# Decode attention over a 512 MiB cache: from a ring of six 32 KiB slots to a ring of three 64 KiB slots

## The chip, the cores and the metric

One core of a Trainium2 chip; the other cores are idle. Its engines go by short names here: PE (TensorE, matrix products), DVE (VectorE), ACT (ScalarE), Pool (GpSimd) and SP (SyncE, which issues the transfers). A descriptor is one contiguous piece of a transfer; the trace shows each as a packet, with its size and its time on one of the 16 DMA engines. A transfer has landed when the last of these engines has counted up its semaphore, the counter that the other engines wait for.

The metric is the device time of one execution in microseconds (us), median of several. Executions of one kernel in one session agree within 0.2%. "Span" is the profile's time from the first to the last instruction, some 2 us less than the device time.

## The reference, cut to what matters

One token, 32 heads, 32768 cached positions of 128 values in bf16. K and V are 256 MiB each; all weights together are about 17 MB.

```python
def reference(A_x, A_k_cache, A_v_cache, A_wq, A_wo, B_x, B_w_gate, B_w_up, B_w_down):
    ...
    xn = _layernorm(x, axis=-1)
    # per head: scores = q . k * Dh**-0.5; p = softmax(scores); o = p . v; then o @ wo
    return x + _A_ref(xn, A_k_cache, A_v_cache, A_wq, A_wo) + _B_ref(xn, B_w_gate, B_w_up, B_w_down)
```

## The kernel before

The cache streams through a ring of slots in SBUF. Partition p holds positions 256 p to 256 p + 255 of a head, 64 KiB of contiguous memory for K and as much for V. SP issues the transfers in order, each as soon as its slot's last user is done:

```python
    CH = 128                      # positions of a partition in one slot: 32 KiB
    NCH = NJ // CH                # 2 slots per head of K, 2 of V
    SLOTS = 6
    SCR = 2                       # score buffers
    TAIL = [64, 32, 16, 16]       # the last V slot comes in four pieces
    ...
                for u in units:   # wq, ffn, then k and v alternating, wo, the last v
                    s = slot_of[u]
                    for o in ([s] if u[0] in ("k", "v") else [s, s + 1]):
                        if o in owner:
                            e.wait_ge(*owner.pop(o))
                    ...
                    elif u[0] == "k":
                        _, h, c = u
                        e.dma_start(ring[:, s, :], kv_src(A_k_cache, h, c * CH, CH)).then_inc(s_slot[s], 16)
                        owner[s] = (s_qk, NHF * (h * NCH + c + 1))
```

The DVE multiplies K by q in place, 64 positions at a time. The PE sums groups of the 128 products by matmuls with an identity matrix, the DVE reduces the rest. After the last chunk of a head the DVE takes the maximum, the PE transposes and spreads it, and ACT does the exp. The PE's order:

```python
                for k in range(NK):
                    scores(k)
                    h, c = divmod(k, NCH)
                    if c < NCH - 1:
                        if h >= 1:
                            total(h - 1)          # denominator of the previous head
                            pv(h - 1, c)          # its V chunk
                        continue
                    if h >= 1:
                        halves = pv_ops(h - 1, c)
                        next(halves)              # first half of the V chunk
                    turn(h)                       # transpose of the maximum
                    if h >= 1:
                        next(halves)              # second half
                    spread(h)
                    if h >= 2:
                        fold(h - 2)
                fold(H - 2)
                t.wait_ge(s_wo, 16)
                t.wait_ge(s_ov, H - 1)
                for h in range(H - 1):
                    att(h)                        # output projection, 5 matmuls per head
                total(H - 1)
                for c in range(NCH):
                    pv(H - 1, c)                  # last V: 256 matmuls of one column
                t.wait_ge(s_ov, H)
                att(H - 1).then_inc(s_att, 1)
```

## Time and profile before

| | before |
|---|---|
| median time | 1302.45 us (1302.35 to 1302.62) |
| span of the profiled run | 1300.05 us |
| PE busy, DVE busy | 81%, 52% |
| rate of transfers, 100 to 1100 us | 431 to 432 GB/s |
| last data landed, from the start | 1295.44 us |
| from there to the end | 4.61 us |

The page of the kernel before: the span; the busy share of the 16 DMA engines in 40 slices, in tenths; what they moved; the packets; the queue's share of the engines' time.

```profile
span 1300.1 us, 9523 instructions
...
DMA  9999999999999999999999999999999999999997
GB/s 396 428 426 435 433 429 428 433 435 427 435 429 434 427 433 431 432 429 433 432 432 425 434 433 431 431 430 436 428 430 432 433 430 429 433 432 430 429 407 315
DMA packets 23960, 554.60 MB, mean 427 GB/s; under 512 B 2480, under 2 KB 6640, under 8 KB 6896
...
q1 hardware_dynamic: 23920, 554.00, 99.5%
```

The engines that carry the transfers are busy in every slice until the last, and 99.5% of their time goes to the one queue. While every engine is busy, the stream can end sooner only if its packets take less time in all. The chain that ended last, by engine and by line:

```profile
DMA 51%; PE 32%; DVE 16%; SPq 1%; issue 0%; DVEq 0%; ACT 0%
DMA ring<-in_A_k_cache_dram 47%; PE ps L233 18%; DVE ring L488 15%; PE ps L279 10%; DMA ring<-in_B_w_down_dram 2%; DMA ring<-in_A_v_cache_dram 2%; PE ps L250 2%; PE ps L330 1%; PE ps L321 0%; SPq L190 0%; PE ps L315 0%; PE ps L338 0%; SPq L185 0%; SPq L195 0%; DVE sc L496 0%
```

The DVE and PE steps in this chain are how a slot comes free for the next transfer. They do not slow the stream here, because the queue holds several transfers: in the packet records at least 15 packets are in flight at any time between 60 and 1240 us. Two groups of instructions (busy us, mean ns of one | idle before, and what ended it):

```profile
L488 DVE TENSOR_TENSOR ring<-ring,qb 128x8192 bf16<-128x8192 bf16 x128 | 560.6, 4421 | 117.0 <-DMA ring<-in_A_k_cache_dram 117.0
...
L279 PE MATMUL ps<-ring,P 128*4 128x512 bf16 x1984 | 443.3, 379 | 0.0
```

The DVE waits 117 us in all for K. That is the sign of compute with time to spare.

The end of the timeline (start, duration, engine, line; in brackets the idle time before and what ended it). It shows the last V's 256 matmuls and the issue of the output:

```profile
1285.74 3.55 PE L275 MATMUL ps<-P,ring 128*128 128x1 bf16 x128 [3.02 <-DMA ring<-in_A_v_cache_dram]
...
1290.57 1.01 PE L275 MATMUL ps<-P,ring 128*128 128x1 bf16 x32 [1.28 <-DMA ring<-in_A_v_cache_dram]
...
1292.20 1.86 PE L275 MATMUL ps<-P,ring 128*128 128x1 bf16 x64 [0.61 <-issue]
...
1295.49 0.58 PE L275 MATMUL ps<-P,ring 128*128 128x1 bf16 x16 [0.65 <-DMA ring<-in_A_v_cache_dram]
...
1296.98 0.35 SPq L202 DMA_DIRECT2D out_dram<-outb  x1
```

The PE follows the last pieces as they land, and the output leaves 1.54 us after the last of them (1296.98 - 1295.44).

The trace also records every packet's size and duration. In the kernel before:

```text
bytes    4096   8192   16384   17280   32768   40960
ns        159    309     611     644    1216    1514     (median)
```

### The profile page before, as it was taken

The numbers are of one execution on the slowest core, as the hardware profiler recorded it, in microseconds if no ns is written. First come the engines' busy times: TensorE is split into PE (matmuls) and PEld (weight loads), VectorE is DVE, ScalarE is ACT, GpSimd is POOL, SyncE is SP. The second block draws the span as 40 slices with busy tenths as digits, with TensorE's granted clock in tenths as the row PEclk, the third lists the DMA queues.
The fourth block names the chain that finished last, engine by engine and source line by source line (L and its number), as shares of the span: only waits on it lengthen the run. The fifth ranks groups of instructions, "written<-read, shape, count | busy, mean of one in ns | idle before, by whom it ended". The sixth has DMA issues, their size and how long they took to land.

```text
span 1300.1 us, 9523 instructions
## 1 busy us (share of the span) xinstructions
PE 1056.5 (81%) x5142; PEld 261.4 (20%) x3222; DVE 678.1 (52%) x406; ACT 50.8 (4%) x139; POOL 1.1 (0%) x8
## 2 busy tenths in 40 slices
PE   3678888888887887887887887887887888878886
PEld 1311122211212211211211211211211211212215
DVE  0465566456455466456455455455456455456450
ACT  2000000000000000000000000000000000000000
POOL 0000000000000000000000000000000000000000
PEclk9689899988989989889988899988899998989996
DMA  9999999999999999999999999999999999999997
GB/s 396 428 426 435 433 429 428 433 435 427 435 429 434 427 433 431 432 429 433 432 432 425 434 433 431 431 430 436 428 430 432 433 430 429 433 432 430 429 407 315
DMA packets 23960, 554.60 MB, mean 427 GB/s; under 512 B 2480, under 2 KB 6640, under 8 KB 6896
## 3 DMA queue, kind: packets, MB, share of 16 engines
q1 hardware_dynamic: 23920, 554.00, 99.5%
q8 instruction: 33, 0.54, 0.2%
q14 instruction: 7, 0.06, 0.0%
HBM read 553.99 MB, written 0.00 MB: 426 GB/s over the span
## 4 chain that ended last, share of the span: by engine, by line
DMA 51%; PE 32%; DVE 16%; SPq 1%; issue 0%; DVEq 0%; ACT 0%
DMA ring<-in_A_k_cache_dram 47%; PE ps L233 18%; DVE ring L488 15%; PE ps L279 10%; DMA ring<-in_B_w_down_dram 2%; DMA ring<-in_A_v_cache_dram 2%; PE ps L250 2%; PE ps L330 1%; PE ps L321 0%; SPq L190 0%; PE ps L315 0%; PE ps L338 0%; SPq L185 0%; SPq L195 0%; DVE sc L496 0%
## 5 line engine op out<-in xcount | busy, mean ns | idle before, releaser
L488 DVE TENSOR_TENSOR ring<-ring,qb 128x8192 bf16<-128x8192 bf16 x128 | 560.6, 4421 | 117.0 <-DMA ring<-in_A_k_cache_dram 117.0
L233 PE MATMUL ps<-ring,ident 128*128 128x512 bf16 x1920 | 508.6, 425 | 0.0
L279 PE MATMUL ps<-ring,P 128*4 128x512 bf16 x1984 | 443.3, 379 | 0.0
L279 PEld LDWEIGHTS ps<-ring,P 128*4 128x4 bf16 x1984 | 163.4, 85 | 346.7 <-issue 109.4
L250 PE MATMUL ps<-ring,ident 128*128 128x512 bf16 x128 | 55.7, 435 | 209.0 <-DVE ring L488 209.0
L496 DVE TENSOR_REDUCE sc<-ps 128x64 f32<-128x512 f32 x128 | 88.3, 690 | 243.8 <-PE ps L233 243.8
L250 PEld LDWEIGHTS ps<-ring,ident 128*128 128x128 bf16 x128 | 12.6, 98 | 518.8 <-DVE ring L488 421.5
L412 ACT ACTIVATE P<-sc,negb 128x256 bf16<-128x256 f32 x32 | 16.3, 508 | 1186.1 <-DVE negb L511 1186.1
L511 DVE TENSOR_SCALAR negb<-ps 128x1 f32<-128x1 f32 x32 | 5.0, 158 | 108.4 <-PE ps L321 108.4
L506 DVE TENSOR_REDUCE m<-ps 1x1 f32<-1x128 f32 x32 | 8.9, 279 | 81.6 <-PE ps L315 81.6
L309 PEld LDWEIGHTS ps<-rsum,ones 128*128 128x128 f32 x64 | 12.3, 194 | 104.8 <-issue 104.0
L300 PE MATMUL ps<-identf,o 4*128 4x1 f32 x248 | 31.8, 245 | 0.9 <-ACT o L395 0.9
L300 PEld LDWEIGHTS ps<-identf,o 4*128 4x128 f32 x248 | 30.0, 187 | 0.9 <-ACT o L395 0.9
L225 PE MATMUL ps<-ring 128*128 128x512 bf16 x40 | 11.5, 461 | 11.9 <-DMA ring<-in_A_wq_dram 11.9
L395 ACT ACTIVATE o<-ps,rzb 4x512 f32<-4x512 f32 x31 | 21.0, 677 | 0.0
L457 DVE TENSOR_SCALAR sg<-sg 128x13 f32<-128x13 f32 (+1 forms) x2 | 0.2, 158 | 35.0 <-ACT sg L388 35.0
L503 DVE TENSOR_REDUCE pmax<-sc 128x1 f32<-128x256 f32 x32 | 13.4, 420 | 1.1
L315 PE MATMUL ps<-identf,pmax 128*1 128x128 f32 x64 | 12.2, 272 | 1.2 <-DVE pmax L503 1.2
L321 PE MATMUL ps<-m,ones 1*128 1x1 f32 x64 | 12.1, 256 | 0.4 <-DVE m L506 0.4
L330 PE MATMUL ps<-xn,ring 128*128 128x1 bf16 (+1 forms) x140 | 8.8, 198 | 4.4 <-DMA ring<-in_B_w_down_dram 4.4
L275 PE MATMUL ps<-P,ring 128*128 128x1 bf16 x256 | 7.6, 165 | 5.7 <-DMA ring<-in_A_v_cache_dram 5.1
L321 PEld LDWEIGHTS ps<-m,ones 1*128 1x128 f32 x64 | 9.4, 182 | 14.2 <-issue 13.5
(47 smaller groups left out, 85.7 us busy)
## 6 DMA issues: line engine op xcount, KB each, us to landing
ring<-in_A_k_cache_dram SPq DMA_DIRECT2D x64, 4096.0 KB, 44.5
ring<-in_A_v_cache_dram SPq DMA_DIRECT2D x63, 4096.0 KB, 47.1
ring<-in_A_wq_dram SPq DMA_DIRECT2D x1, 5120.0 KB, 15.5
ring<-in_A_wo_dram SPq DMA_DIRECT2D x1, 5120.0 KB, 43.0
ring<-in_B_w_gate_dram SPq DMA_DIRECT2D x1, 2160.0 KB, 20.2
ring<-in_B_w_up_dram SPq DMA_DIRECT2D x1, 2160.0 KB, 24.8
ring<-in_B_w_down_dram SPq DMA_DIRECT2D x1, 2080.0 KB, 28.6
ring<-in_A_v_cache_dram SPq DMA_DIRECT2D x1, 2048.0 KB, 21.3
```

Source lines behind the costliest of these rows:

```text
L233: return t.add_instruction(mybir.InstMatmult(start_tensor_calc=False, stop_tensor_calc=stop, tile_size=(128, 128), tile_position=(0, 0), l ...
L250: t.matmul(ob, lhsT=ident[:, :], rhs=src, start=True, stop=False)
L279: mm = t.matmul(O[h % 2], lhsT=P[:, h % PR, jj:jj + W], rhs=ring[:, s, j * DH:(j + W) * DH], start=(jj == 0), stop=(jj + W == NJ))
L300: mm = t.matmul(fold_ps, lhsT=o4[:, m * DH:(m + 1) * DH], rhs=identf[0:W, m:m + 1], start=(m == 0), stop=(m == W - 1))
L309: t.matmul(misc[:, 129:130], lhsT=ones[:, :], rhs=rsum[:, h % SR:h % SR + 1], start=True, stop=True).then_inc(s_z, 1)
L321: t.matmul(misc[:, 128:129], lhsT=ones[0:1, :], rhs=m1[0:1, h % SR:h % SR + 1], start=True, stop=True).then_inc(s_b, 1)
L330: mm = t.matmul(misc[0:n, off + j:off + j + 1], lhsT=hidden(w, c, j), rhs=xn[:, c:c + 1], start=(c == 0), stop=(c == NCD - 1))
L395: a.activation(out=o4[:, :], in_=O[h % 2], func=ACTF.Copy, scale=rzb[0:W, h % SR:h % SR + 1]).then_inc(s_o4, 1)
L412: a.activation(out=P[:, h % PR, :], in_=sc[:, h % SCR, :], func=ACTF.Exp, bias=negb[:, h % SR:h % SR + 1], scale=c_scale, accum_out=rsum[: ...
L488: v.tensor_tensor(out=kh, in0=kh, in1=q[:, None, :].to_broadcast([128, HF, DH]), op=ALU.mult).then_inc(s_mul, 1)
L496: v.tensor_reduce(out=sc[:, h % SCR, j:j + HF], in_=bank[n % NBK].rearrange("p (j e) -> p j e", e=G), axis=AX.X, op=ALU.add).then_inc(s_re ...
L503: v.tensor_reduce(out=pmax[:, h % SR:h % SR + 1], in_=sc[:, h % SCR, :], axis=AX.X, op=ALU.max).then_inc(s_max, 1)
```

## The change

Intent: fewer, larger transfers. One slot now holds a whole head of K or of V, so each partition's 64 KiB is one descriptor and there are half as many. The ring's size stays (3 x 64 KiB), the order of the stream stays. Weights take one slot instead of two. The second score buffer goes, and total(h - 1) moves ahead of the V products.

```diff
-    CH = 128
+    CH = NJ
...
-    SLOTS = 6
+    SLOTS = 3
...
-    SCR = 2
+    SCR = 1
...
-    TAIL = [64, 32, 16, 16]
+    TAIL = [128, 64, 32, 16, 16]
...
-    pos = 0
-    for u in units:
-        wide = 1 if u[0] in ("k", "v") else 2
-        assert wide == 1 or pos % 2 == 0
+    for pos, u in enumerate(units):
         s = pos % SLOTS
         slot_of[u] = s
-        pos += wide
...
                     if h >= 1:
+                        if NCH == 1:
+                            total(h - 1)
                         halves = pv_ops(h - 1, c)
                         next(halves)
                     turn(h)
```

More of the change, by code (lines that the diff above doesn't have):

```diff
@@ L134, in bass_parallel_sum__gqa_block_cached__swiglu_ffn__decode_kernel @@
         xnb = flat[:, x0:x0 + NCD * 128].rearrange("p (c m) -> p c m", c=NCD)
-        assert NCD * (H * DH + 128) <= 2 * CE
+        assert NCD * (H * DH + 128) <= CE
         wq_v = wq.rearrange("p (c n) -> p c n", c=NCD)
@@ L141, in bass_parallel_sum__gqa_block_cached__swiglu_ffn__decode_kernel @@
         wd = flat[:, d0:d0 + FB * D].rearrange("p (j d) -> p j d", j=FB)
-        assert 2 * NCD * F + FB * D <= 2 * CE
+        assert 2 * NCD * F + FB * D <= CE
         wg_v = wg.rearrange("p (c n) -> p c n", c=NCD)
@@ L152, in bass_parallel_sum__gqa_block_cached__swiglu_ffn__decode_kernel @@
         wo_v = wo.rearrange("p h (m c) -> p h m c", c=NCD)
-        assert H * D <= 2 * CE and NCD * H * DH <= 2 * CE
+        assert H * D <= CE
         def kv_src(cache, h, j0, n):
@@ L171, in sp @@
                     s = slot_of[u]
-                    for o in ([s] if u[0] in ("k", "v") else [s, s + 1]):
-                        if o in owner:
-                            e.wait_ge(*owner.pop(o))
+                    if s in owner:
+                        e.wait_ge(*owner.pop(s))
                     if u[0] == "wq":
                         e.dma_start(wq, A_wq.rearrange("(p c) n -> p (c n)", c=NCD)).then_inc(s_wq, 16)
-                        owner[s] = owner[s + 1] = (s_q, NQB)
+                        owner[s] = (s_q, NQB)
                     elif u[0] == "k":
@@ L197, in sp @@
                         e.dma_start(wd[0:FL, FM, :], B_w_down[FM * 128:F, :]).then_inc(s_ffn, 16)
-                        owner[s] = owner[s + 1] = (s_fpd, 1)
+                        owner[s] = (s_fpd, 1)
                     else:
```

## The prediction

> **What bounds the kernel now.** The transfers. The profile's DMA row reads nine tenths in 39 of 40 slices, queue 1 holds 99.5% of the 16 engines' span, and the rate is 430 to 433 GB/s in every 100 us from 100 to 1200 us (stage table). The chain of waits is 47% K transfers. Compute has room: PE 81%, DVE 52%. In the timeline two heads take 77.7 us (DVE product at 1174.3 and 1252.0), 38.86 us per head of 16.8 MB. Where the data is already there (113.4 to 148.4 us) a head takes 35.0 us.
>
> **What it removes.** In the trace's packet records a descriptor's time is a straight line: 4096 B 159 ns, 8192 B 309, 16384 B 611, 17280 B 644, 32768 B 1216 (fastest 1211), 40960 B 1514. The slope is 27.2 bytes/ns per engine, the intercept 8 to 9 ns. The Trainium skill, "DMA: Bandwidth & Descriptors", section "Where 436 GB/s comes from", gives 435.2 GB/s for 16 ports, the same 27.2 each; this trace agrees. So the bytes are at the ceiling and only the fixed 8.5 ns per descriptor, plus 9 ns per semaphore write, can be saved. 16,256 descriptors of 32 KiB become about 8,130: per engine 500 x 8.5 ns = 4.3 us, and 60 semaphore writes x 9 ns = 0.6 us. Expected gain 5 us, 0.4%, all on the critical path. A 64 KiB descriptor should take about 2418 ns (estimate from the line) against 2 x 1216.
>
> **What it moves.** Estimated loop of one head after, from the product's start: four products 17.5 us, the PE step after the last 3.6, denominator 0.4, first half of PV 7.1, transpose 0.3, second half 7.1, spread and bias 0.6: 36.6 us, against 38.7 between K landings. Slower than 35.0, because the DVE no longer multiplies under the first PV, but 2 us under the transfers. V lands 19.4 us after K, the PE wants it at 21.6: no new wait on average. A K slot comes free 21 us after it landed and is wanted after 39; a V slot after 17, wanted after 39. The queue never runs empty; some 15 us of backlog are tolerated. The single score buffer waits for an exp that ended before the next K landed: free.
>
> **Ends.** The first K lands at about 52 us instead of 42, but the engines stay busy meanwhile. At the end the PE leaves the last whole PV later (36.6 us after K31 landed); the output projection (6.4 us) ends at 47 us, the first V31 piece lands at 44, the last at 54. 256 products at 28 ns are 7.1 us: the tail may grow by 0.3 to 1 us.
>
> **Prediction.** 1302.45 - 4.9 + 0.5 = 1298 us; 8 times in 10 within 1295 to 1302. Chances: faster by over 2% 0.01, within 2% 0.96, slower 0.03.
>
> **What would show it.** K packets of 65,536 B at about 2418 ns; DMA rate about 433 GB/s in the middle; heads 38.7 us apart; DVE waits for K of 1 to 3 us once per head; first product at about 52 us; tail after the last landing within 1 us of now.
>
> **What would make it wrong.** A 64 KiB row cut into smaller descriptors (no gain, about 1302). PE steps slowed: its granted clock falls to 0.66 after idle gaps, and 2 us more per head would make compute the bound (each us past 38.7 costs 30 us). V landing late under the PE's in-order wait, which would hold back the transpose, the bias and the next head's products.

## The result, and the profile after

Median 1299.47 us (1299.21 to 1299.63, 4 runs), before 1302.5 us in the same session (the three runs above and a fourth of 1302.55). The ratio is 0.9977, 95% interval 0.9959 to 0.9994. Ratios here are the mean time of one kernel's runs over that of the other's of the same rounds, so not quite the ratio of the medians.

| | before | after |
|---|---|---|
| median time | 1302.5 us | 1299.47 us |
| span | 1300.05 | 1297.31 |
| last data landed | 1295.44 | 1290.41 |
| from there to the issue of the output | 1.54 | 3.33 |
| from that issue to the end | 3.07 | 3.57 |
| first K product | 46.25 | 52.42 |
| from head to head, mean of heads 10 to 30 | 39.01 | 38.86 |

The same lines of the page, after:

```profile
span 1297.3 us, 9428 instructions
...
DMA  9999999999999999999999999999999999999997
GB/s 399 435 434 425 441 431 435 428 435 431 441 425 433 433 436 431 427 439 427 447 421 435 435 427 445 421 443 426 435 435 427 443 423 439 429 438 429 433 395 288
DMA packets 14887, 554.59 MB, mean 427 GB/s; under 512 B 1472, under 2 KB 5632, under 8 KB 5888
...
q1 hardware_dynamic: 14848, 554.00, 99.2%
```

There are 9073 packets fewer, and the rate in the middle is 432 to 434 GB/s instead of 431 to 432 (table of stages, 200 us each). The slices swing more (421 to 447); a packet is now 2.4 us long, and with packets of 0.6 us (split4, below) the slices stay within 426 to 429. In the packet records 8064 packets of 65,536 bytes have a median of 2421 ns. The chain, and the two groups:

```profile
DMA 52%; PE 30%; DVE 15%; issue 3%; SPq 0%; ACT 0%; DVEq 0%
DMA ring<-in_A_k_cache_dram 52%; PE ps L274 17%; DVE ring L485 14%; PE ps L228 10%; PE ps L245 1%; PE ps L270 1%; PE ps L340 1%; PE ps L310 0%; PE ps L304 0%; PE ps L295 0%; SPq L190 0%; DVE sc L493 0%; PE ps L316 0%; ACT o L392 0%; SPq L192 0%
```

```profile
L485 DVE TENSOR_TENSOR ring<-ring,qb 128x8192 bf16<-128x8192 bf16 x128 | 557.8, 4419 | 91.6 <-DMA ring<-in_A_k_cache_dram 91.6
...
L274 PE MATMUL ps<-ring,P 128*4 128x512 bf16 x1984 | 438.3, 379 | 0.0
```

The DVE's wait for K is now 91.6 us over 30 heads, 3 us each. One head in the middle of the run shows the new order of work:

```profile
732.65 17.43 DVE L485 TENSOR_TENSOR ring<-ring,qb 128x8192 bf16<-128x8192 bf16 x4 [4.26 <-DMA ring<-in_A_k_cache_dram]
...
750.36 3.40 PE L228 MATMUL ps<-ring,ident 128*128 128x512 bf16 x15
...
753.79 0.33 SPq L185 DMA_DIRECT2D ring<-in_A_v_cache_dram  x1
...
753.81 7.07 PE L274 MATMUL ps<-ring,P 128*4 128x512 bf16 x32
...
760.93 7.07 PE L274 MATMUL ps<-ring,P 128*4 128x512 bf16 x32
...
768.35 0.16 DVE L508 TENSOR_SCALAR negb<-ps 128x1 f32<-128x1 f32 x1 [6.93 <-PE ps L316]
...
771.45 17.43 DVE L485 TENSOR_TENSOR ring<-ring,qb 128x8192 bf16<-128x8192 bf16 x4 [2.94 <-DMA ring<-in_A_k_cache_dram]
```

The four products take 17.4 us, the PE step after the last ends at 753.8, and the K slot is given to the next V at 753.79. Then come two halves of V products, and the bias at 768.35. The loop has 2.94 us to spare before the next K lands. The end of the run:

```profile
1282.88 4.62 PE L270 MATMUL ps<-P,ring 128*128 128x1 bf16 x160
...
1290.12 2.72 PE L270 MATMUL ps<-P,ring 128*128 128x1 bf16 x96 [2.62 <-issue]
...
1293.74 0.35 SPq L197 DMA_DIRECT2D out_dram<-outb  x1
```

The data was there: the pieces landed at 1280.56, 1285.50, 1287.92, 1289.16 and 1290.41. Matmul 160 lies in the middle of the second piece, and yet the PE stood still before it for 2.62 us. The transfers gained 5.03 us, and the tail gave back 2.29.

### The profile page after: what moved, and what is told of

Read it like the earlier page. It is cut to its first block, busy times and chain, and to the rows that moved or that the text cites. A ratio compares the mean times of both kernels' runs of the same rounds, so it can differ in the third digit from the quotient of the medians.

```text
span 1297.3 us, 9428 instructions
## 1 busy us (share of the span) xinstructions
PE 1036.7 (80%) x5142; PEld 263.8 (20%) x3222; DVE 669.7 (52%) x406; ACT 50.8 (4%) x139; POOL 1.1 (0%) x8
## 4 chain that ended last, share of the span: by engine, by line
DMA 52%; PE 30%; DVE 15%; issue 3%; SPq 0%; ACT 0%; DVEq 0%
DMA ring<-in_A_k_cache_dram 52%; PE ps L274 17%; DVE ring L485 14%; PE ps L228 10%; PE ps L245 1%; PE ps L270 1%; PE ps L340 1%; PE ps L310 0%; PE ps L304 0%; PE ps L295 0%; SPq L190 0%; DVE sc L493 0%; PE ps L316 0%; ACT o L392 0%; SPq L192 0%
## 5 line engine op out<-in xcount | busy, mean ns | idle before, releaser
L485 DVE TENSOR_TENSOR ring<-ring,qb 128x8192 bf16<-128x8192 bf16 x128 | 557.8, 4419 | 91.6 <-DMA ring<-in_A_k_cache_dram 91.6
L228 PE MATMUL ps<-ring,ident 128*128 128x512 bf16 x1920 | 495.3, 416 | 0.0
L274 PE MATMUL ps<-ring,P 128*4 128x512 bf16 x1984 | 438.3, 379 | 0.0
L245 PE MATMUL ps<-ring,ident 128*128 128x512 bf16 x128 | 56.2, 439 | 228.8 <-DVE ring L485 228.6
L274 PEld LDWEIGHTS ps<-ring,P 128*4 128x4 bf16 x1984 | 166.1, 85 | 245.3
L493 DVE TENSOR_REDUCE sc<-ps 128x64 f32<-128x512 f32 x128 | 82.2, 683 | 62.1 <-PE ps L228 62.1
L473 DVE RECIPROCAL rzb<-ps 128x1 f32<-128x1 f32 x32 | 5.0, 157 | 9.8 <-PE ps L304 9.8
```

The source lines that it names most:

```text
L228: return t.add_instruction(mybir.InstMatmult(start_tensor_calc=False, stop_tensor_calc=stop, tile_size=(128, 128), tile_position=(0, 0), l ...
L245: t.matmul(ob, lhsT=ident[:, :], rhs=src, start=True, stop=False)
L274: mm = t.matmul(O[h % 2], lhsT=P[:, h % PR, jj:jj + W], rhs=ring[:, s, j * DH:(j + W) * DH], start=(jj == 0), stop=(jj + W == NJ))
L485: v.tensor_tensor(out=kh, in0=kh, in1=q[:, None, :].to_broadcast([128, HF, DH]), op=ALU.mult).then_inc(s_mul, 1)
L493: v.tensor_reduce(out=sc[:, h % SCR, j:j + HF], in_=bank[n % NBK].rearrange("p (j e) -> p j e", e=G), axis=AX.X, op=ALU.add).then_inc(s_re ...
```

## The experiments

Eleven kernels, all correct, all built from the changed one.

### 1. Is it the descriptors? Cutting the loads again

The slots stay; only the load of a slot is cut. split2, split4 and split16 use PARTS = 2, 4, 16 transfers of 32, 16 and 4 KiB per partition:

```diff
-    e.dma_start(ring[:, s, :], kv_src(A_k_cache, h, c * CH, CH)).then_inc(s_slot[s], 16)
+    for i in range(PARTS):
+        n = CH // PARTS
+        e.dma_start(ring[:, s, i * n * DH:(i + 1) * n * DH],
+                    kv_src(A_k_cache, h, c * CH + i * n, n)).then_inc(s_slot[s], 16)
...
-    v.wait_ge(s_slot[s], 16 * use_of[u])
+    v.wait_ge(s_slot[s], 16 * PARTS * use_of[u])
```

(The same for V and the PE's wait.) stride2 has the descriptors of split4 in the number of transfers of split2, because each transfer takes every other piece:

```diff
+    for b in range(2):
+        e.dma_start(ring[:, s, :].rearrange("p (a b n) -> p b a n", a=2, b=2)[:, b],
+                    kv_src(A_k_cache, h, c * CH, CH).rearrange("p (a b n) -> p b a n", a=2, b=2)[:, b]
+                    ).then_inc(s_slot[s], 16)
```

Expected of split2:

> The changed kernel with its three 64 KiB slots, but each 8 MiB load issued as two transfers of 32 KiB per partition. Theory A (the gain is the fixed time of each descriptor): per engine and load 16 x 1213 + 2 x 9 ns = 19.43 us against 19.35 now, over 63 loads +4.6 us: last V landing back at about 1295 us from the start, time about 1304 us, which is slower than the kernel before, because the longer tail (6.9 us after the last landing, 4.6 before) stays. Theory B (the gain comes from the slots or from fewer waits of the queue): heads stay 38.70 us apart, time about 1299.5.

Of split4:

> The same with four transfers of 16 KiB per partition. Theory A: per engine and load 32 x 611 + 4 x 9 ns = 19.59 us, +0.235 us over 63 loads = +14.8 us: time about 1314. Theory B: about 1299.5. Theory C (the fixed cost is that of a transfer and its semaphore, not of a descriptor): from two to four transfers adds as much again as from one to two did.

Of stride2:

> Two transfers per 8 MiB load, each of which carries every other 16 KiB piece of a partition: as many transfers as split2, as many and as large descriptors as split4. Theory A: about 1.1 us less than split4, time about 1313. Theory C (cost per transfer): as split2, about 1304.

Of split16:

> Sixteen transfers of 4 KiB per partition for each load. Theory A: 128 x 159 + 16 x 9 ns = 20.50 us per load, +1.15 us over 63 loads = +72 us: time about 1371, heads about 41.0 us apart. Any theory without a cost per descriptor: below 1310. If the sequencer cannot issue sixteen transfers in 20 us (16 x 0.33 to 0.44 us = 5 to 7 us, estimate), the transfers would show gaps and the time would be above 1390.

Measured (before: 1302.21 us, timed beside these four):

| kernel | descriptor | transfers per load | packet, median | last landing | time | ratio to before |
|---|---|---|---|---|---|---|
| changed | 64 KiB | 1 | 2421 ns | 1290.41 us | 1299.47 us | 0.9977 |
| split2 | 32 KiB | 2 | 1216 ns | 1295.50 us | 1303.44 us | 1.0011 |
| split4 | 16 KiB | 4 | 614 ns | 1305.15 us | 1313.01 us | 1.0083 |
| stride2 | 16 KiB | 2 | 615 ns | 1305.02 us | 1312.82 us | 1.0082 |
| split16 | 4 KiB | 16 | 162 ns | 1361.02 us | 1367.57 us | 1.0502 |

The rate by slices of split4, then of split16 with its packets:

```profile
GB/s 388 427 428 427 429 426 428 427 429 427 428 427 427 427 428 428 428 427 428 427 429 427 428 428 426 428 427 429 427 428 428 428 427 427 429 428 426 429 403 300
```

```profile
GB/s 386 409 410 409 409 409 409 410 409 410 409 410 408 409 409 410 409 409 409 410 409 409 410 409 409 409 410 409 410 409 409 410 409 409 410 409 409 409 399 319
DMA packets 150975, 554.72 MB, mean 406 GB/s; under 512 B 16592, under 2 KB 20752, under 8 KB 150032
```

Theory A holds over a range of sixteen. Each of the 63 loads has 8 descriptors per engine in the changed kernel, so split2 adds 8 x 63 = 504 to each engine and split16 adds 120 x 63 = 7560. The last landing moves by 5.09 and 70.61 us, which is 10.1 and 9.3 ns per descriptor; split4 gives 14.74 / 1512 = 9.7 ns. Theory B falls: with three slots and 32 KiB descriptors the last V lands at 1295.50, where the kernel before had it (1295.44). So the ring of three slots neither gained nor cost anything in the stream. Theory C falls: stride2 lies with split4 (0.2 us apart), not with split2. The share I gave to semaphore writes, 9 ns each, should have put stride2 1.1 us under split4; 0.13 us at the last landing is all that shows. Within that, the fixed time belongs to the descriptor.

### 2. Is the compute loop really off the critical path?

Idle matmuls on a free PSUM bank, between the transpose and the second half of V, n = 7 or 18 per head:

```diff
+    for i in range(n):
+        if i == 0:
+            t.matmul(bank[0], lhsT=ident[:, :], rhs=qb[:, 0:512], start=True, stop=False)
+        else:
+            again(bank[0], ident[:, :], qb[:, 0:512], i == n - 1)
     next(halves)
```

> The changed kernel with 7 idle 128x512 matmuls per head behind the transpose, about 1.5 us of PE time (7 x 0.216 us). Theory A (transfers bound it; the loop of a head, 35.9 us in the trace, has nearly 3 us to spare against 38.8): heads stay 38.9 us apart, last landing unchanged at 1290.4 us; only the tail, which starts from the PE's last head, may grow by up to 1.5 us: time 1299.3 to 1301. Theory P (the PE loop is the bound already, or late heads block the three slots): 31 x 1.5 = 46 us more.

> The same with 18 idle matmuls, 3.9 us per head: loop 35.9 + 3.9 = 39.8 us, now over the transfers. Theory A: heads about 39.8 us apart, first product still at 52.4 us, time about 1330 (1322 to 1336), waits of the DVE for K near zero.

slow7: 1301.23 us (before, timed beside it, 1302.42; ratio 0.9991, 0.9976 to 1.0006). slow18: 1335.38 us (1.0254). The line of the waits on K (us in total, times, longest), first of slow7, then of slow18:

```profile
DVE ring L490 <- DMA ring<-in_A_k_cache_dram: 40.6, 27, 6.8
```

```profile
DVE ring L490 <- DMA ring<-in_A_k_cache_dram: 6.2, 1, 6.2
```

With 1.5 us more per head, the heads stay 38.857 us apart, to the last digit as in the changed kernel, and the DVE's waits for K shrink from 91.6 to 40.6 us: the work went into the idle time. With 3.9 us more, the heads are 39.88 us apart (39.8 was expected) and only the very first K is still waited for. The margin of some 3 us per head is shown from both sides. The numbers agree: 3.9 us more per head cost 1.02 us, so 2.9 us were to spare. The time of slow7 lies 0.2 us above what was expected, and its last piece landed at 1292.56 us, not at 1290.4: a miss. That piece came 2.8 us after the one before it (1.25 us in the changed kernel), while a 16 KiB packet of instructions was in transit from 1289.8; this link is argued, not tested. It did not set the time, for the PE reached the last piece later still:

```profile
1285.18 4.60 PE L270 MATMUL ps<-P,ring 128*128 128x1 bf16 x164
1292.13 2.61 PE L270 MATMUL ps<-P,ring 128*128 128x1 bf16 x92 [2.35 <-issue]
```

The added work and a later last head made the PE start its last burst 2.30 us later (1285.18 against 1282.88), and the run ended 2.02 us later. The stop of the changed kernel's tail is here too, 4 matmuls further on; the next section says why.

### 3. What holds up the tail?

Two theories for the 2.3 us that the tail lost. L is the prediction's: the PE comes out of its last whole V late. F: the PE runs through one-column matmuls faster than its program arrives. The Trainium skill, "Runtime: NRT & Kernel Launch", section "Instruction fetch mechanics", says that an engine's program is refilled in blocks of 16 KiB, 256 instructions, by the sequencer's own transfers. A one-column matmul with its weight load is two instructions, so a block is 128 of them. The trace agrees in size for the PE: 33 packets of 16,384 bytes on the instruction queue q8. (The other instruction queue, q14, has packets of 8,192 bytes.) One of those on q8 starts at 1287.7 us in the changed kernel, and the stop ends at 1290.12.

The test moves the block boundaries, without changing the work, by idle matmuls early in the PE's program, where it waits for weights anyway (n = 32 or 64):

```diff
+    for _ in range(n):
+        t.matmul(misc[:, 200:201], lhsT=ident[:, :], rhs=ident[:, 0:1], start=True, stop=True)
     t.wait_ge(s_ffn, 64)
```

> The changed kernel with 32 idle matmuls early in the PE's program (before the FFN, where it waits 5 us), which shift all later PE instructions by 4 KiB of program text. The PE stood still for 2.6 us in the tail at matmul 160 of the last V's 256, with nothing to wait for, until just after a 16 KiB instruction packet landed. Theory F (the tail's PE burst outruns the fetch of its instructions, 128 matmuls with their weight loads per 16 KiB packet): the stop moves to matmul 128, the next boundary is at the end of the burst; last product about 0.7 us earlier, time 1298.5 to 1299.5. Theory L (the tail is long because the PE comes out of the last whole V late, as predicted): no stop moves, time unchanged at 1299.5, plus or minus 0.2.

> The same with 64 idle matmuls. Theory F: stops at matmuls 96 and 224 of the last 256, together about 4 us, time about 1300.5. Theory L: unchanged, 1299.5, one stop or none at 160.

Times: pad32 1298.49 us (ratio 0.9972, 0.9959 to 0.9984), pad64 1299.69 us (0.9982, 0.9968 to 0.9996); before 1302.27. The last V's matmuls in the timeline, pad32 and then pad64:

```profile
1283.22 3.55 PE L270 MATMUL ps<-P,ring 128*128 128x1 bf16 x128
1288.77 3.57 PE L270 MATMUL ps<-P,ring 128*128 128x1 bf16 x128 [2.00 <-issue]
```

```profile
1284.61 2.70 PE L270 MATMUL ps<-P,ring 128*128 128x1 bf16 x96
1289.23 3.57 PE L270 MATMUL ps<-P,ring 128*128 128x1 bf16 x128 [1.92 <-issue]
1293.23 1.01 PE L270 MATMUL ps<-P,ring 128*128 128x1 bf16 x32 [0.43 <-issue]
```

The stop moved from matmul 160 to 128 and to 96, exactly by the number of matmuls put in thousands of instructions earlier. No theory about data or lateness does that, so it is shown that the stop lies at a block boundary of the program, as F says. In pad64 the second stop at 224 is there too, but it is short (0.43 us), and the total fell short of the 4 us that I expected. The differences in time to the changed kernel (timed in another session), -1.0 and +0.2 us, have the sign and rough size of F's, but the intervals of the ratios overlap; the moved stop is the evidence, not the times.

Kernels made for other questions agree. split2, split4 and stride2 leave the PE's program as it is, and stop before matmul 160 (2.62, 2.35 and 2.62 us). slow7 adds 31 x 8 = 248 instructions (7 matmuls and a weight load per head), 8 fewer than a block, so its boundary comes 4 matmuls later: it stops before 164. slow18 has no stop at all:

```profile
1322.23 6.96 PE L270 MATMUL ps<-P,ring 128*128 128x1 bf16 x256
```

There the data had all landed (1315.79 us) before the burst began, and the packets of q8 start 3.9 us apart in the burst, against 6.1 us in the changed kernel, whose transfers were still running. So the PE outruns its program here because the program comes slowly, and it seems to come slowly because of the stream of data; no run tests this second step alone.

The other half: let the PE start its last burst sooner. early2 projects heads 0 to 29 ahead of the fold of head 30, and head 30 behind the last V:

```diff
+    fold_last = ps8[:, 0, 8:9]        # fold of head 30, and its copy to ocol, use this bank
...
-                fold(H - 2)
                 t.wait_ge(s_wo, 16)
-                t.wait_ge(s_ov, H - 1)
-                for h in range(H - 1):
+                t.wait_ge(s_ov, H - 2)
+                for h in range(H - 2):
                     att(h)
+                fold(H - 2)
                 total(H - 1)
                 for c in range(NCH):
                     pv(H - 1, c)
+                t.wait_ge(s_ov, H - 1)
+                att(H - 2)
                 t.wait_ge(s_ov, H)
```

(Also a wait of the DVE for s_ov 31 before its last column, which keeps the semaphore's order unambiguous.)

> The changed kernel with the output projection of heads 0 to 29 put ahead of the fold of head 30 (whose sum moves to a free PSUM bank), and that of head 30 put behind the last V. The PE starts its last burst about 2 us earlier (1274.2 instead of 1276.2). Theory L: the burst ends about 1 us earlier or meets the last landing at 1290.4, tail 1 to 1.8 us shorter, time about 1298. Theory F: the fetches also start earlier, so the end moves by up to 2 us, and a stop of about 2.5 us remains somewhere in the burst, at a spacing of 128 matmuls from the other boundaries.

> Both edits together. Theory F: another 0.5 us, time about 1297.5, the last product waits for the last V landing. Theory L: as early2 alone.

early2: 1298.19 us (0.9969, 0.9957 to 0.9982). Both edits: 1298.32 us (0.9970, 0.9957 to 0.9982), where 1297.5 was expected: a miss. The timeline of early2:

```profile
1282.96 4.54 PE L271 MATMUL ps<-P,ring 128*128 128x1 bf16 x165
1289.43 2.59 PE L271 MATMUL ps<-P,ring 128*128 128x1 bf16 x91 [1.93 <-issue]
```

The burst did not start sooner (1282.96 against 1282.88): the fold had only moved into it. So the test of L failed, and early2's time is near the 1298 of theory L without L's reason. What did change is that att(30) left the instructions ahead of the burst, and the stop moved by its 5 matmuls, from 160 to 165; it is still 1.93 us long. With both edits it shrinks to 0.82 us and the PE again waits for the last piece, as in the kernel before, yet the time is no better than with either edit alone. The record shows why:

```profile
1287.51 3.01 PE L271 MATMUL ps<-P,ring 128*128 128x1 bf16 x107 [0.82 <-issue]
1290.89 0.58 PE L271 MATMUL ps<-P,ring 128*128 128x1 bf16 x16 [0.38 <-DMA ring<-in_A_v_cache_dram]
1291.34 0.34 PE L343 MATMUL ps<-ocol,ring 128*128 128x1 bf16 x5
1292.61 0.36 PE L343 MATMUL ps<-ocol,ring 128*128 128x1 bf16 x5 [0.93 <-DVE ocol L520]
```

The stop lies before matmul 133, so the next boundary is 128 later, after all 256 and att(30)'s 5, just before att(31). There the PE stood still for another 0.93 us. The view names the DVE, but that one had been done since 1291.74, 0.87 us before; a packet of q8 had started at 1290.03, some 2.6 us before the PE went on. The edit had moved one stop behind the last product. Both kernels beat the kernel before; early2 has the lowest median of all. Against the changed kernel its gain of 1.3 us lies within the intervals and was measured on another chip.

No run made the burst start sooner, so it stays untested what an earlier start would bring. slow7 shows the other direction: a burst 2.30 us later, with a stop no longer than before, ended the run 2.02 us later.

### 4. What spreads the 16 engines?

Each transfer counts 16 increments of its semaphore. The Trainium skill, "DMA: Bandwidth & Descriptors", section "Why a DMA increments its semaphore by 16 and not by 1", says that these are one for each engine. The trace has their times, so it shows how far the engines are apart: 1.25 us between the first and the last at 32 us, 6.48 us at 1257 us, 5.07 us at the last landing of the changed kernel. The kernel before is alike (5.10). The sum of the 16 delays grows from 5.3 to 55.8 us between these two points, in steps: about 1.5 us for each 16 KiB packet of instructions that was moved in between, 0.8 us for each of 8 KiB, and none in loads without such a packet. Theory S: such a packet holds up one engine, and nothing evens this out, because the queue is never empty. The test adds program text to the Pool, which has nothing to do:

```diff
+    for _ in range(16000):            # some 8,000 instructions, about 512 KB
+        g.wait_ge(s_const, 4)
```

> The changed kernel with some 8,000 waits that are already met in the idle Pool engine's program (about 512 KB of program text, as much as the PE's). Theory S (each fetch of a packet of instructions holds up one of the 16 DMA engines by 1 to 1.5 us, and nothing evens the engines out, so that the last engine ends 5 us after the first): the sum over the engines of the delays to the first, 44 us at the last landing now, grows by 30 to 50 us; the last landing and the time move by 1 to 5 us (1300.5 to 1304). Rival (the spread comes from the memory or from the transfers themselves): sum of delays and time unchanged within 0.3 us.

Measured: 1333.94 us (1331.85 to 1334.37; ratio 1.0239). The rate of this kernel by slices, and its queue of instruction packets; then that queue in the changed kernel:

```profile
GB/s 389 439 438 434 428 430 432 434 430 432 408 409 387 411 430 407 395 411 410 438 383 410 412 440 429 421 437 418 437 433 429 433 435 428 433 437 431 428 343 259
...
q14 instruction: 69, 0.57, 0.1%
```

```profile
q14 instruction: 6, 0.05, 0.0%
```

That such packets hold up an engine is shown, but my size was wrong by a factor of ten (1 to 5 us expected). The 63 packets more, of 8 KiB, hold up one engine alone: in the load of 263.6 us 15 engines are within 2.1 us of the first and one is 15.9 us behind. The largest delay rises by about 1.3 us per load, in which mostly two of these packets start, until it stands at about 20 us from 340 us on, while the sum of the delays stays below 35 us. From then on a slot is not free until that one engine has finished with it, and the other 15 wait for it: 20.5 us per load between 116 and 711 us, against 19.35 us. The rate drops to 383 to 412 GB/s in most slices from 11 to 23, and it recovers when the Pool has run through its waits (its last packet of the series starts at 715.9 us). No run gave the Pool the same waits without the program text; that one engine alone is late speaks for the packets. The end moves by 34.5 us. The expectation that the sum of delays grows by 30 to 50 us failed with it: at the last landing the sum is 9.7 us, since the waiting had evened out the rest.

## Why the prediction was right

The measured 1299.47 us lies in the range (1295 to 1302), in the middle class as forecast, 1.5 us above the 1298.

1. "What bounds the kernel now": right. Transfers before and after; slow7 and slow18 show the margin.
2. "What it removes": right in kind and size. A 64 KiB descriptor takes 2421 ns (2418 predicted). The last landing came 5.03 us earlier (4.9 predicted). Two parts are to be mended: the semaphore writes add next to nothing (stride2 against split4), and the descriptor's fixed time is 9 to 10 ns in the landings where the line of packet times gives 8.5. The first error took 0.6 us too much, the second 0.7 us too little, so that the sum fits this closely is partly luck.
3. "What it moves": the loop is 35.9 us (732.65 to 768.51 in the timeline shown), not 36.6, so the margin is nearly 3 us and not 2. The queue never ran empty: split2, with the same slots, lands with the kernel before. "Some 15 us of backlog are tolerated" was near: in the last experiment one engine lagged about 20 us before the stream slowed.
4. Heads "38.7 us apart": 38.86 on average. Most heads are 38.7 us apart, as each engine needs 19.35 us per load. But a K counts as landed when its slowest engine is done, and three times in the run this one fell back by about 1.5 us: three steps from head to head took 40.1 to 40.2 us. The kernel before has the same drift (39.01), so the difference, 0.152 us x 32 heads = 4.9 us, is as predicted.
5. "Ends": the term that was mis-sized. Predicted +0.3 to 1 us from a PE that comes late; measured +2.29. The PE did come late enough to run 155 + 2 + 160 matmuls without a wait, but the loss up to the issue of the output, 1.79 us, comes from the 2.62 us stop for instructions, which the pads moved about: without it 256 products of 28 ns from 1282.88 would have met the last landing at 1290.41 (an estimate). In the kernel before only 0.61 us of the stop showed, it seems because the waits of 3 us for V ahead of matmul 0 and of 1.28 us ahead of matmul 128 gave the fetch time. The other 0.50 us of the loss came after that issue (3.57 against 3.07 us): 0.14 us until the output had landed and 0.36 us from there to the end, for which I have no reason.

## What to carry to other kernels

When the DMA engines are busy from end to end, plot packet time against packet size: the intercept times the number of descriptors per engine that go is what larger descriptors won here. It was 0.4% of the stream (5.03 us), because a 32 KiB descriptor takes 1216 ns of which only some 9 are fixed, and the tail left 0.2% of the time. Here fewer slots cost nothing, since every slot came free before the queue wanted it; check this by adding idle work until the time moves. A tail of one-column matmuls can be bound by the arrival of the program itself: if a stop has no releaser, shift the program by a few instructions and see whether the stop shifts too.

## What the Trainium skill lacked or had wrong

- "Runtime: NRT & Kernel Launch", section "Instruction fetch mechanics", calls crossing a block boundary "mostly hidden". In bursts of one-column matmuls it was not: stops of 2.62, 2.00 and 1.92 us at the block boundary (changed kernel, pad32, pad64), each ending about 2.4 to 2.5 us after the packet started; with no data in transfer (slow18) it was hidden. The page gives blocks of 16 KiB for any engine; the packets that the Pool's program added on q14 are of 8 KiB.
- No page that I read says how much these fetches hold up the data. "DMA: Bandwidth & Descriptors", section "Queues, rings and completion order", says only that each DMA engine takes turns between its queues, the runtime's refills among them. Here a 16 KiB packet delayed one of the 16 engines by about 1.5 us, the engines were 5 us apart at the end (mean delay 44.5 / 16 = 2.8 us, so about 2.3 us are lost by an estimate from these numbers), and 63 packets on one engine cost 34.5 us.
- "DMA: Bandwidth & Descriptors" gives no time per large descriptor; the nearest is about 10.5 ns per packet in section "Bandwidth", from a 4 KB transfer issued by GpSimd. Here it is size / 27.2 bytes per ns plus 8.5 ns in the packet records, 9 to 10 ns in the landings, from 4 to 64 KiB. Its fixed cost of about 2 us per transfer (section "Anatomy of one DMA", for transfers issued by GpSimd) does not show in a full queue of transfers issued by SP: 126 more of them (split4 against stride2) moved the last landing by 0.13 us.
- The same page's largest measured rate is 425 GB/s (section "Bandwidth", 16 MB); here one core held 432 to 434 GB/s for a millisecond, close to the 435.2 that it derives.
